# First chunk of an adaLN block: scale and shift weights in halves of 512 columns, all row tiles transposed ahead of the first query matmul, and the shift of k-tiles 0 to 3 added last, as a bias

## The chip, the cores and the metric

The kernel runs on one core of a Trainium2 chip. The metric is the device time of one execution in microseconds (us); several executions are timed, and the median is quoted. The granted clock is the TensorE clock that the chip's throttle let through, as a share of full speed; in a run at a mean of 0.998 it fell for some microseconds (3.4 in the one that was profiled). TensorE is called PE in the profile, its weight loads PEld, VectorE DVE, ScalarE ACT, GpSimd POOL, and the engine that issues the DMAs SP. SBUF is the core's working memory, PSUM the memory that TensorE writes its results to, in banks.

## The reference, cut to what matters

In an adaLN block the scale and the shift that follow a layer norm are computed from a second input, here `c`.

```python
x = A_x                                           # 2048 rows of 1024, bf16
mod = (silu(c) @ w_mod)                           # six vectors of 1024: sa, ca, ga, sb, cb, gb
h = layernorm(x) * (1 + ca) + sa                  # "scale" is 1 + ca, "shift" is sa
qkv = h @ wqkv                                    # q, k, v; linear attention follows
x = x + ga * (attention(q, k, v) @ wo)
h = layernorm(x) * (1 + cb) + sb
return x + gb * (silu(h @ w_gate) * (h @ w_up) @ w_down)
```

The opening must therefore do this before the large matmuls can run: load x and normalise it, transpose it (the contraction is over the 1024 columns), compute the scale and the shift from 2 MB of weights each, apply both, and multiply by the query weights. The first chunk is 512 rows, that is four row tiles of 128. Its 1024 columns make eight k-tiles of 128.

## The kernel before: the parts that the change and the argument touch

All DMAs of the opening are issued in order on one queue. The scale weights (`wca`) and the shift weights (`wsa`) come in pieces of 256 columns, which makes DMA rows of 512 bytes; x and the query weights have rows of 2 KB.

```python
for p in range(4):
    ca_load(p)            # 256 columns of the scale weights: 512 KB in rows of 512 B
    if p != 2:
        sa_load(p)        # 256 columns of the shift weights
    if p < 3:
        wq_load(p)        # two k-tiles of the query weights: 512 KB in rows of 2 KB
for i in range(6, 8):
    P.dma("wq%d" % i, ...)
sa_load(2)                # the shift of k-tiles 4 and 5 comes last
```

The scale and the shift are made by matmuls of one column (`mod_sc`: eight for each of the eight k-tiles, in PSUM bank 0). The opening works in halves of 256 rows: row tiles 0 and 1 are transposed, scaled and multiplied, then tiles 2 and 3.

```python
def mod_sc(w, c0, ms):
    for m in ms:
        for kt in range(NDT):
            P.pe("matmul", out=PS[:, 0, c0 + m:c0 + m + 1], lhsT=w[:, kt, m * 128:(m + 1) * 128],
                 rhs=SILUC[:, kt:kt + 1], ...)
# ...
mod_sc(WCA, 8, range(2))        # scale of k-tiles 0 and 1
warm(4, bank=3)                 # filler matmuls of 512 columns
# ...
mod_sc(WSA, 0, range(2))        # shift of k-tiles 0 and 1
warm(3, bank=3)
# ... scale and shift h of k-tiles 0 and 1 from PSUM, copy the other k-tiles unscaled to SBUF

def q_phase_chunk0(side):
    for nt in range(5):
        q_part(nt, qb[nt], (0, 1), 0, 256)      # first half of the rows
    tile_transposes(2)
    tile_transposes(3)
    for dt in range(2):
        h0_first(dt, 1, "dve")
    # ... copies; second half; then k-tiles 2 to 7, each with its own scale and shift matmuls ...
            if nt == 5:
                bias_mm()                        # shift of k-tiles 4 and 5 as a bias of q
            q_part(nt, qb[nt], (7,))
    for f in ln_ops[1]:                          # statistics of row tile 5, on VectorE
        f()
```

The last piece, the shift of k-tiles 4 and 5, is not added to h before the query matmuls. Its product with the query weights is a vector, and that is given to the activations that empty the query banks as a bias (`BIASQ`). Before the key matmuls the shift is added to h itself (`h0_shift`), and the k matmuls of chunk 0 take k-tiles 4 and 5 last.

## Time and profile before

| | before |
|---|---|
| median of the timed runs | 836.52 us (836.39 to 836.97, 3 runs) |
| span of the profiled run | 834.2 us |
| TensorE busy | 823.6 us, 99% |
| first query matmul of chunk 0 | 12.53 us |
| weights of the first key matmul of chunk 0 load at | 31.29 us |

The first fence holds lines of the page: busy time of each engine with its share of the span and its instructions, the DMA packets, and the chain that ended last by engine.

```profile
PE 823.6 (99%) x4050; PEld 380.4 (46%) x4129; DVE 304.1 (36%) x676; ACT 197.3 (24%) x339; POOL 42.9 (5%) x56
DMA packets 195085, 117.18 MB, mean 140 GB/s; under 512 B 49624, under 2 KB 178784, under 8 KB 195040
PE 97%; DVE 1%; DMA 1%; issue 1%; SPq 0%; ACT 0%; DVEq 0%
```

TensorE is nearly full, and the chain is TensorE almost everywhere. What can still be won is in the opening. The next fence is the timeline of TensorE alone in the kernel before: start in us, duration in us, engine, line, operation, tiles, shape, count, and in brackets the idle time before it with what ended it.

```profile
12.53 1.38 PE L178 MATMUL ps<-ht,wqk 128*128 128x256 bf16 x10 [0.34 <-DVE ht L178]
13.74 1.06 PE L178 MATMUL ps<-ident,xres 128*128 128x128 bf16 x16
15.09 1.04 PE L178 MATMUL ps<-ht,wqk 128*128 128x256 bf16 x6 [0.28 <-DVE ht L178]
...
24.38 0.55 PE L178 MATMUL ps<-siluc,wsa 128*128 128x1 bf16 x16
...
28.94 0.55 PE L178 MATMUL ps<-modtmp,wqk 128*128 128x1 bf16 x16
29.36 40.89 PE L178 MATMUL ps<-ht,wqk 128*128 128x512 bf16 x183
```

The 16 transposes of row tiles 2 and 3 stand between query matmuls, and TensorE then waits for their scaled copies. From 29 us on the matmuls follow each other every 0.216 to 0.220 us. The weight loads tell more than the matmuls where a wait is short, but they overstate what it costs: in a dense stretch a load stands one matmul (0.216 us) ahead of its own matmul, and a wait up to about that length costs TensorE nothing (at 29.75 us below the loads waited 0.30 us, and the matmuls still followed each other at 0.215). What is lost shows in the starts of the matmuls. This is the timeline of the weight loads before:

```profile
24.38 0.47 PEld L178 LDWEIGHTS ps<-siluc,wsa 128*128 128x128 bf16 x16 [0.53 <-DMA wsa<-in_w_mod_dram]
...
29.75 2.73 PEld L178 LDWEIGHTS ps<-ht,wqk 128*128 128x128 bf16 x14 [0.30 <-DVE biasq L178]
32.84 0.10 PEld L178 LDWEIGHTS ps<-ht,wqk 128*128 128x128 bf16 x1 [0.37 <-DVE ht L178]
33.11 0.98 PEld L178 LDWEIGHTS ps<-ht,wqk 128*128 128x128 bf16 x6 [0.17 <-DVE ht L178]
```

At 24.38 us they wait for a piece of shift weights, at 29.75 for the copy of the bias (it frees bank 0 for the eighth query group). The first eight loads from 29.75 on are that group; the ninth, at 31.29 us, is the first key matmul. At 32.84 and 33.11 us the first key group waits for the two shifted k-tiles. Its loads come every 0.216 us, so without these waits the one at 33.11 would have come at 31.29 + 7 x 0.216 = 32.80: it is 0.31 us late. The two shifts come late because they stand on VectorE behind statistics of row tile 4, which wait for ScalarE. At 46 us there is a similar wait: the first query matmuls of the second chunk need h that VectorE is scaling just then, after a DMA has transposed it.

```profile
32.12 0.22 DVE L178 SCALAR_TENSOR_TENSOR mv<-sumx,sumsq 128x1 f32<-128x1 f32 x1 [0.74 <-ACT ht L178]
...
32.45 0.61 DVE L178 TENSOR_SCALAR ht<-ht,modcol 128x512 bf16<-128x512 bf16 x2
...
44.46 2.67 DVE L178 TENSOR_SCALAR ht<-ht,modcol 128x512 bf16<-128x512 bf16 x8 [0.34 <-DMA ht<-xres]
```

```profile
47.19 1.84 PEld L178 LDWEIGHTS ps<-ht,wqk 128*128 128x128 bf16 x10 [0.23 <-DVE ht L178]
```

The last fence of before shows the traffic of the opening from 6 to 24 us: window and its length, busy time of PE, PEld, DVE, ACT and POOL with instructions, granted TensorE clock, DMA busy share, GB/s.

```profile
6.00:24.00 18.00, 17.07 (x188) 10.09 (x189) 10.28 (x44) 7.17 (x12) 2.24 (x4) 1.00 1.13 322
```

The DMA engines are busy throughout (a share above 1 means that packets overlap) and move 322 GB/s.

### The profile page before, as it was taken

Reading aid. Unit: us, or ns where it says so; the run is one execution under the profiler, and the core shown is the slowest. Engines: PE = TensorE matmul, PEld = TensorE weight load, DVE = VectorE, ACT = ScalarE, POOL = GpSimd, SP = SyncE. Lnnn points to the kernel's source line nnn. Section 1 sums busy time; section 2 is a strip of 40 time slices with the busy share of each in tenths; the row PEclk is TensorE's granted clock in tenths of the full one; section 3 lists DMA queues with packets and bytes.
Section 4 is the critical chain, followed back from the end, with each engine's and each line's share of the span. In section 5 each row is a group of like instructions: output and inputs, shape, how many; then the busy total and the mean of one; then the engine's idle time right before and its main releaser. Section 6 shows DMA issues by size and latency. Waiting matters only on the chain.

```text
span 834.2 us, 10048 instructions
## 1 busy us (share of the span) xinstructions
PE 823.6 (99%) x4050; PEld 380.4 (46%) x4129; DVE 304.1 (36%) x676; ACT 197.3 (24%) x339; POOL 42.9 (5%) x56
## 2 busy tenths in 40 slices
PE   8999999999999999999999999999999999999998
PEld 4444444454444444444444444444444444444444
DVE  6698975757974211110222212022111212111111
ACT  4568642213332111110211111011111111111011
POOL 1000000000050000030000003000000300000000
PEclk9999999999999999999999999999999999999999
DMA  9969734928197895620455571045557104553000
GB/s 278 308 151 223 213 91 146 201 101 302 26 228 227 262 281 152 169 52 19 114 152 152 151 183 45 13 114 152 152 152 193 34 13 117 154 152 95 1 26 25
DMA packets 195085, 117.18 MB, mean 140 GB/s; under 512 B 49624, under 2 KB 178784, under 8 KB 195040
## 3 DMA queue, kind: packets, MB, share of 16 engines
q1 hardware_dynamic: 195040, 116.55, 51.0%
q8 instruction: 32, 0.52, 0.3%
q14 instruction: 13, 0.11, 0.0%
HBM read 100.67 MB, written 4.33 MB: 126 GB/s over the span
## 4 chain that ended last, share of the span: by engine, by line
PE 97%; DVE 1%; DMA 1%; issue 1%; SPq 0%; ACT 0%; DVEq 0%
PE ps L178 97%; DMA wsa<-in_w_mod_dram 1%; DVE acc L178 0%; SPq L178 0%; DVE xres L178 0%; DVE mhl L178 0%; DVE ht L178 0%; ACT mw L178 0%; DVE modtmp L178 0%; DVE ve L178 0%; DVE ut L178 0%; DVE modcol L178 0%; DVE mean L178 0%; DVE msq L178 0%; DVE sumx L178 0%
## 5 line engine op out<-in xcount | busy, mean ns | idle before, releaser
L178 PE MATMUL ps<-h2t,guu 128*128 128x512 bf16 x878 | 210.1, 379 | 0.9
L178 PE MATMUL ps<-h2t,gug 128*128 128x512 bf16 x878 | 209.9, 379 | 0.9
L178 DVE TENSOR_TENSOR at<-sg,ps 128x512 bf16<-128x512 bf16 x112 | 77.0, 688 | 296.2 <-PE ps L178 285.1
L178 ACT ACTIVATE sg<-ps 128x512 bf16<-128x512 f32 x112 | 67.0, 598 | 310.2 <-PE ps L178 298.5
L178 PEld LDWEIGHTS ps<-h2t,guu 128*128 128x128 bf16 x896 | 87.7, 98 | 105.7
L178 PEld LDWEIGHTS ps<-h2t,gug 128*128 128x128 bf16 x896 | 87.5, 98 | 105.3
L178 PE MATMUL ps<-ht,wqk 128*128 128x512 bf16 (+1 forms) x510 | 112.2, 375 | 1.4 <-DVE ht L178 0.6
L178 PE MATMUL ps<-wd_a,at 128*128 128x512 bf16 (+2 forms) x519 | 112.8, 372 | 0.5
L178 PE MATMUL ps<-wd_b,at 128*128 128x512 bf16 (+2 forms) x388 | 85.4, 372 | 0.5
L178 PEld LDWEIGHTS ps<-wd_a,at 128*128 128x128 bf16 x528 | 51.1, 98 | 59.8
L178 PEld LDWEIGHTS ps<-ht,wqk 128*128 128x128 bf16 x522 | 49.8, 98 | 60.4 <-DVE ht L178 2.6
L178 DVE TENSOR_TENSOR ut<-att,gb_b 128x512 bf16<-128x512 bf16 (+1 forms) x32 | 14.0, 438 | 167.1 <-ACT att L178 167.1
L178 ACT ACTIVATE att<-ps 128x512 bf16<-128x512 f32 (+1 forms) x32 | 17.4, 591 | 182.1 <-PE ps L178 182.1
L178 PEld LDWEIGHTS ps<-wd_b,at 128*128 128x128 bf16 x396 | 38.3, 98 | 44.7
L178 PE MATMUL ps<-pk,xres 128*128 128x512 bf16 x249 | 56.2, 379 | 0.5 <-issue 0.2
L178 PE MATMUL ps<-mw,pqt 128*128 128x512 bf16 x250 | 55.8, 379 | 0.4
L178 POOL TENSOR_SCALAR h2t<-h2t,modcol 128x512 bf16<-128x512 bf16 x32 | 28.5, 909 | 393.9 <-DMA h2t<-xn 377.6
L178 ACT ACTIVATE e<-ps 128x512 bf16<-128x512 f32 x56 | 33.0, 604 | 31.4 <-PE ps L178 21.9
L178 PEld LDWEIGHTS ps<-mw,pqt 128*128 128x128 bf16 x256 | 24.9, 98 | 29.7 <-DVE xres L178 0.2
L178 PEld LDWEIGHTS ps<-pk,xres 128*128 128x128 bf16 x256 | 24.7, 98 | 29.8 <-issue 0.4
L178 ACT ACTIVATE junk<-xres 128x1024 bf16<-128x1024 bf16 x24 | 25.4, 1059 | 36.0 <-DVE xres L178 35.8
L178 POOL TENSOR_TENSOR rstd<-ve,neghalf 128x1 f32<-128x1 f32 (+2 forms) x17 | 13.7, 817 | 217.3 <-DVE ve L178 176.6
(101 smaller groups left out, 347.7 us busy)
## 6 DMA issues: line engine op xcount, KB each, us to landing
gug<-in_B_w_gate_dram SPq DMA_DIRECT2D x56, 512.0 KB, 4.0
guu<-in_B_w_up_dram SPq DMA_DIRECT2D x56, 512.0 KB, 5.3
xres<-in_A_x_dram SPq DMA_DIRECT2D x20, 256.0 KB, 6.9
rb<-recip_den SPq DMA_DIRECT2D x8, 512.0 KB, 11.4
stgx<-in_w_mod_dram SPq DMA_DIRECT2D x2, 2048.0 KB, 8.7
wd_a<-in_B_w_down_dram SPq DMA_DIRECT2D x4, 1024.0 KB, 7.5
out_dram<-xres SPq DMA_DIRECT2D x31, 128.0 KB, 1.7
xres<-in_A_x_dram SPq DMA_DIRECT2D x3, 1024.0 KB, 14.5
```

Of the source, the lines that this page charges most:

```text
L178: return getattr(e, method)(**kw)
```

## The change

The intent is to hand TensorE longer pieces of work and the DMA engines longer rows. The scale and shift weights come in halves of 512 columns (rows of 1 KB); the scale of k-tiles 0 to 3 is computed at once; all four row tiles are transposed ahead of the first query matmul; in k-tiles 0 to 3, h is first scaled only, 512 rows at a time, straight from PSUM. The shift of k-tiles 0 to 3 is loaded last and enters q as a bias, and the key matmuls of chunk 0 begin with k-tiles 4 to 7. The statistics of row tiles 4 and 5 also come earlier in the program. Cut to its core:

```diff
-        for p in range(4):
-            ca_load(p)
-            if p != 2:
-                sa_load(p)
-            if p < 3:
-                wq_load(p)
-        # ... wq 6, wq 7, sa_load(2)
+        ca_load(0)            # now 512 columns: 1 MB in rows of 1 KB
+        wq_load(0, 2)
+        ca_load(1)
+        wq_load(2, 2)
+        sa_load(1)
+        # ... wq_load(4) to wq_load(7)
+        sa_load(0)
 # (cut) bias_mm:
-                for dt in (4, 5):
+                for dt in range(4):
 # (cut) opening:
-        mod_sc(WCA, 8, range(2))
         warm(4, bank=3)
 # (cut) row tile 3: statistics wholly on VectorE instead of half on ScalarE
-        mod_sc(WSA, 0, range(2))
-        warm(3, bank=3)
+        mod_sc(WCA, 8, range(4))
+        fin_ca(0, 4)
+        tile_transposes(2, 3)
+        h0_first(0, "dve")    # 512 rows each, scale only
+        h0_first(1, "dve")
+        h0_first(2, "dve")
+        h0_first(3, "dve")
+        raw_copy(4)           # ScalarE, 1024 wide
+        raw_copy(6)
 # (cut) after the shift of k-tiles 6 and 7: act_stats(4), the statistics of row tile 4, which stood behind k-tile 7
 # (cut) k_group:
-            for i, dt in enumerate((0, 1, 2, 3, 6, 7, 4, 5) if ch == 0 else range(NDT)):
+            for i, dt in enumerate((4, 5, 6, 7, 0, 1, 2, 3) if ch == 0 else range(NDT)):
 # (cut) q_phase_chunk0, k-tile 7:
+                if nt == 0:
+                    mod_sc(WSA, 0, range(4))
+                    fin_sa(0, 4, True)
+                    for f in ln_ops[1]:
+                        f()
+                    ln1_rstd1(5)
+                if nt == 4:
+                    bias_mm()
 # (cut)
-            for dt in (4, 5):
+            for dt in range(4):
                 h0_shift(dt)
```

More of the change, by code (lines that the diff above doesn't have):

```diff
@@ L399, in ca_load, with wq_load @@
         def ca_load(p):
-            P.dma("wca%d" % p, WCA[:, :, 256 * p:256 * p + 256], wmv[:, :, D + 256 * p:D + 256 * p + 256])
-        def wq_load(p):
-            P.dma("wqp%d" % p, WQK[:, 2 * p:2 * p + 2, 0:D], wqkvv[:, 2 * p:2 * p + 2, 0:D])
+            P.dma("wca%d" % p, WCA[:, :, 512 * p:512 * p + 512], wmv[:, :, D + 512 * p:D + 512 * p + 512])
         def sa_load(p):
-            P.dma("wsa%d" % p, WSA[:, :, 256 * p:256 * p + 256], wmv[:, :, 256 * p:256 * p + 256])
-        for p in range(4):
-            ca_load(p)
-            if p != 2:
-                sa_load(p)
-            if p < 3:
-                wq_load(p)
-        for i in range(6, 8):
-            P.dma("wq%d" % i, WQK[:, i, 0:D], wqkvv[:, i, 0:D])
-        sa_load(2)
+            P.dma("wsa%d" % p, WSA[:, :, 512 * p:512 * p + 512], wmv[:, :, 512 * p:512 * p + 512])
+        def wq_load(i, n=1):
+            P.dma("wq%d" % i, WQK[:, i:i + n, 0:D], wqkvv[:, i:i + n, 0:D])
+        ca_load(0)
[3 more added lines that the diff above has]
+        sa_load(1)
+        wq_load(4)
+        wq_load(5)
+        wq_load(6)
+        wq_load(7)
+        sa_load(0)
         for j in range(2):
             P.dma("x1_%d" % j, XRES[:, 4 + j, :], xv[:, 4 + j, :])
-        for i in range(2):
+        for i in (1, 0):
             P.dma("wk0%d" % i, WQK[:, 4 * i:4 * i + 4, 1024:1536], wqkvv[:, 4 * i:4 * i + 4, 1024:1536])
@@ L508, in mod_sc, with fin_ca, fin_sa @@
                     mod_first[0] = False
-        def fin_ca(p):
-            sl, sp = slice(2 * p, 2 * p + 2), slice(8 + 2 * p, 10 + 2 * p)
-            return [
-                lambda: P.dve("tensor_copy", out=MODTMP[:, sp], in_=PS[:, 0, sp]),
-                lambda: P.dve("tensor_copy", out=MODTMP[:, sl], in_=PS[:, 0, sl]),
-                lambda: P.dve("tensor_scalar", out=MODTMP[:, sp], in0=MODTMP[:, sp], scalar1=1.0, scalar2=None,
-                              op0=ALU.add),
-                lambda: P.dve("tensor_copy", out=MODCOL[:, 1, sl], in_=MODTMP[:, sl]),
-                lambda: P.dve("tensor_copy", out=MODCOL[:, 0, sl], in_=MODTMP[:, sp]),
-            ]
-        def mv_pair(p):
-            mod_sc(WCA, 8, range(2 * p, 2 * p + 2))
-            mod_sc(WSA, 0, range(2 * p, 2 * p + 2))
-        def mod_pair(p):
-            mv_pair(p)
-            for f in fin_ca(p):
-                f()
-            for dt in range(2 * p, 2 * p + 2):
-                h0_scale(dt)
-        def h0_scale_only(dt):
-            P.dve("tensor_scalar", out=HT[:, 0, dt, :], in0=HT[:, 1, dt, :], scalar1=MODCOL[:, 0, dt:dt + 1],
-                  scalar2=None, op0=ALU.mult)
+        def fin_ca(m, n):
+            P.dve("tensor_scalar", out=MODCOL[:, 0, m:m + n], in0=PS[:, 0, 8 + m:8 + m + n], scalar1=1.0, scalar2=None,
+                  op0=ALU.add)
+        def fin_sa(m, n, cast=False):
+            if cast:
+                P.dve("tensor_copy", out=MODTMP[:, m:m + n], in_=PS[:, 0, m:m + n])
+            P.dve("tensor_copy", out=MODCOL[:, 1, m:m + n], in_=PS[:, 0, m:m + n])
         def h0_shift(dt):
@@ L541, in bias_mm, with h0_first, raw_copy @@
             for nt in range(NDT):
-                for dt in (4, 5):
+                for dt in range(4):
                     P.pe("matmul", out=PS[:, 0, 16 + nt:17 + nt], lhsT=WQK[:, dt, nt * 128:(nt + 1) * 128],
-                         rhs=MODTMP[:, dt:dt + 1], start=False, stop=(dt == 5), skip_group_check=True)
+                         rhs=MODTMP[:, dt:dt + 1], start=False, stop=(dt == 3), skip_group_check=True)
             P.dve("tensor_copy", out=BIASQ[:], in_=PS[:, 0, 16:24])
         def t_view(dt, n=1):
-            return PSB[:, 6 + dt // 4, (dt % 4) * 256:(dt % 4 + n) * 256]
-        def h0_first(dt, half, eng):
-            dst = HT[:, 0, dt, 256 * half:256 * half + 256]
+            return PSB[:, 4 + dt // 2, (dt % 2) * 512:(dt % 2 + n) * 512]
+        def h0_first(dt, eng):
             if eng == "act":
-                P.act("activation", out=dst, in_=t_view(dt), func=ACT.Identity, scale=MODCOL[:, 0, dt:dt + 1],
-                      bias=MODCOL[:, 1, dt:dt + 1])
-            else:
-                P.dve("tensor_scalar", out=dst, in0=t_view(dt), scalar1=MODCOL[:, 0, dt:dt + 1],
-                      scalar2=MODCOL[:, 1, dt:dt + 1], op0=ALU.mult, op1=ALU.add)
-        def raw_copy(dt, n, half, eng):
-            dst = HT[:, 1, dt:dt + n, 256 * half:256 * half + 256]
-            src = t_view(dt, n).rearrange("p (d q) -> p d q", q=256)
-            if eng == "act":
-                P.act("activation", out=dst, in_=src, func=ACT.Copy)
-            else:
-                P.dve("tensor_copy", out=dst, in_=src)
+                P.act("activation", out=HT[:, 0, dt, :], in_=t_view(dt), func=ACT.Copy, scale=MODCOL[:, 0, dt:dt + 1])
+            else:
+                P.dve("tensor_scalar", out=HT[:, 0, dt, :], in0=t_view(dt), scalar1=MODCOL[:, 0, dt:dt + 1],
+                      scalar2=None, op0=ALU.mult)
+        def raw_copy(dt):
+            P.act("activation", out=HT[:, 1, dt:dt + 2, :], in_=t_view(dt, 2).rearrange("p (d q) -> p d q", q=512),
+                  func=ACT.Copy)
         def h0_scale(dt):
@@ L607, in neg_rstd, with tile_transposes @@
             P.pool("tensor_tensor", out=RSTD[:, st:st + 1], in0=VE[:, st:st + 1], in1=NEGHALF[:, 0:1], op=ALU.pow)
-        def mixed_mv_ops(st):
-            return [
-                lambda: P.dve("bn_aggr", out=MV[:, st, :], in_=STATS[:, (st // 4) % 2, st % 4, 0:1, :]),
-                lambda: P.dve("scalar_tensor_tensor", out=MSQ2[:, st:st + 1], in0=MV[:, st, 0:1], scalar=MV[:, st, 0:1],
-                              in1=MV[:, st, 1:2], op0=ALU.mult, op1=ALU.add),
-                lambda: P.dve("scalar_tensor_tensor", out=MV[:, st, 0:1], in0=MV[:, st, 0:1], scalar=0.5,
-                              in1=SUMX[:, st:st + 1], op0=ALU.mult, op1=ALU.add),
-                lambda: P.dve("scalar_tensor_tensor", out=SUMSQ[:, st:st + 1], in0=MSQ2[:, st:st + 1], scalar=0.5,
-                              in1=SUMSQ[:, st:st + 1], op0=ALU.mult, op1=ALU.add),
-                lambda: P.dve("scalar_tensor_tensor", out=MV[:, st, 1:2], in0=MV[:, st, 0:1], scalar=MV[:, st, 0:1],
-                              in1=SUMSQ[:, st:st + 1], op0=ALU.mult, op1=ALU.subtract),
-            ]
         act_stats(2)
-        act_stats(3, 512)
         s0_, s1_, s3_ = ln1_stats_ops(0), ln1_stats_ops(1), ln1_stats_ops(3)
-        m2, m3 = act_mv_ops(2), mixed_mv_ops(3)
-        def tile_transposes(j):
+        m2 = act_mv_ops(2)
+        def tile_transposes(*js):
             for dt in range(NDT):
-                c = (dt % 4) * 256 + (j % 2) * 128
-                P.pe("transpose", out=PSB[:, 6 + dt // 4, c:c + 128], in_=XRES[:, j, dt * 128:(dt + 1) * 128],
-                     identity=IDENT[:])
-        fa = fin_ca(0)
+                for j in js:
+                    c = (dt % 2) * 512 + j * 128
+                    P.pe("transpose", out=PSB[:, 4 + dt // 2, c:c + 128], in_=XRES[:, j, dt * 128:(dt + 1) * 128],
+                         identity=IDENT[:])
         warm(13, bank=3)
@@ L648, in bass_adaLN_cond__linear_attn_block__swiglu_ffn__prompt_kernel @@
         tile_transposes(1)
-        warm(0, bank=3)
-        mod_sc(WCA, 8, range(2))
         warm(4, bank=3)
@@ L653, in bass_adaLN_cond__linear_attn_block__swiglu_ffn__prompt_kernel @@
         m2[0]()
-        m3[0]()
         neg_rstd(2)
-        m3[1]()
-        m3[2]()
-        fa[0]()
+        s3_[1]()
+        s3_[2]()
+        ln1_rstd1(3)
         ln1_xn(2)
-        fa[2]()
-        m3[3]()
-        fa[4]()
-        m3[4]()
-        mod_sc(WSA, 0, range(2))
-        warm(3, bank=3)
-        neg_rstd(3)
-        fa[1]()
-        raw_copy(4, 4, 0, "act")
-        fa[3]()
-        h0_first(0, 0, "dve")
-        h0_first(1, 0, "dve")
-        raw_copy(2, 2, 0, "dve")
-        ln1_xn(3)
+        ln1_xn(3)
+        mod_sc(WCA, 8, range(4))
+        fin_ca(0, 4)
+        tile_transposes(2, 3)
+        warm(0, bank=3)
+        h0_first(0, "dve")
[4 more added lines that the diff above has]
+        raw_copy(6)
+        P.act("activation", out=ACTWARM[:], in_=SILUC[:], func=ACT.Exp)
         phi_ctr = [0]
@@ L706, in phi_flush, with q_part @@
             phi_pend.clear()
-        def q_part(nt, bank, dts, c0=0, c1=512):
+        def q_part(nt, bank, dts):
             for dt in dts:
-                P.pe("matmul", out=PS[:, bank, c0:c1], lhsT=WQK[:, dt, nt * 128:(nt + 1) * 128],
-                     rhs=HT[:, 0, dt, c0:c1], start=(dt == 0 and c0 == 0), stop=(dt == 7), skip_group_check=True)
+                P.pe("matmul", out=PS[:, bank, :], lhsT=WQK[:, dt, nt * 128:(nt + 1) * 128],
+                     rhs=HT[:, 0, dt, :], start=(dt == 0), stop=(dt == 7))
         qk_ctr = [0]
@@ L769, in q_phase_chunk0 @@
         def q_phase_chunk0(side):
-            qb = [1, 2, 3, 4, 5, 6, 7]
-            for nt in range(5):
-                q_part(nt, qb[nt], (0, 1), 0, 256)
-            tile_transposes(2)
-            tile_transposes(3)
-            for dt in range(2):
-                h0_first(dt, 1, "dve")
-            raw_copy(4, 4, 1, "act")
-            raw_copy(2, 2, 1, "dve")
-            P.act("activation", out=ACTWARM[:], in_=SILUC[:], func=ACT.Exp)
-            for nt in range(5):
-                if nt == 3:
-                    mod_pair(1)
-                q_part(nt, qb[nt], (0, 1), 256, 512)
@@ L784, in q_phase_chunk0 @@
-            for nt in range(5, 7):
-                q_part(nt, qb[nt], (0, 1))
-            f2, f3 = fin_ca(2), fin_ca(3)
-            for nt in range(7):
-                if nt == 4:
-                    mod_sc(WCA, 8, range(4, 6))
-                    for i in (0, 2, 4):
-                        f2[i]()
-                    for dt in (4, 5):
-                        h0_scale_only(dt)
-                q_part(nt, qb[nt], (2, 3))
-            for nt in range(7):
-                if nt == 3:
-                    mod_sc(WCA, 8, range(6, 8))
-                    for i in (0, 2, 4):
-                        f3[i]()
-                if nt == 5:
-                    mod_sc(WSA, 0, range(6, 8))
-                    for i in (1, 3):
-                        f3[i]()
-                    for dt in (6, 7):
-                        h0_scale(dt)
-                q_part(nt, qb[nt], (4, 5))
@@ L807, in q_phase_chunk0 @@
-            for nt in range(7):
-                q_part(nt, qb[nt], (6,))
-            for nt in range(7):
-                if nt == 3:
-                    mod_sc(WSA, 0, range(4, 6))
-                    for i in (1, 3):
-                        f2[i]()
-                if nt == 5:
+            qb = [1, 2, 3, 4, 6, 5, 7]
+            for nts, dts in ((range(6), (0,)), (range(2), (1,)), ((6,), (0, 1)), (range(2, 6), (1,))):
+                for nt in nts:
+                    q_part(nt, qb[nt], dts)
@@ new lines, in q_phase_chunk0 @@
+            mod_sc(WCA, 8, range(4, 8))
+            fin_ca(4, 4)
+            for nt in range(7):
+                if nt == 6:
+                    mod_sc(WSA, 0, range(4, 6))
+                    fin_sa(4, 2)
+                    for dt in (4, 5):
+                        h0_scale(dt)
+                q_part(nt, qb[nt], (2, 3))
+            mod_sc(WSA, 0, range(6, 8))
+            fin_sa(6, 2)
+            for dt in (6, 7):
+                h0_scale(dt)
+            act_stats(4)
+            for dt in (4, 5, 6):
+                for nt in range(7):
+                    q_part(nt, qb[nt], (dt,))
@@ L815, in q_phase_chunk0 @@
+            for nt in range(7):
+                if nt == 0:
[4 more added lines that the diff above has]
+                    ln1_rstd1(5)
+                if nt == 4:
                     bias_mm()
                 q_part(nt, qb[nt], (7,))
-            for f in ln_ops[1]:
-                f()
-            ln1_rstd1(5)
-            q_phi = lambda nt: phi_evac(qb[nt] if nt < 7 else 0, PQT[:, nt, 0:512], bias=BIASQ[:, nt:nt + 1])
@@ L821, in q_phase_chunk0 @@
-            act_stats(4, mid=lambda: q_phi(0))
             for f in act_mv_ops(4):
@@ L824, in q_phase_chunk0 @@
             neg_rstd(4)
-            for i, dt in enumerate((4, 5, 0, 1, 2, 3, 6, 7)):
+            ln1_xn(5)
+            ln1_xn(4)
+            th_dma(5)
+            th_dma(4)
+            q_phi = lambda nt: phi_evac(qb[nt] if nt < 7 else 0, PQT[:, nt, 0:512], bias=BIASQ[:, nt:nt + 1])
+            for i, dt in enumerate(range(NDT)):
                 P.pe("matmul", out=PS[:, 0, :], lhsT=WQK[:, dt, 896:1024], rhs=HT[:, 0, dt, :], start=(i == 0),
                      stop=(i == 7))
-            for dt in (4, 5):
+            for dt in range(4):
                 h0_shift(dt)
             for nt in range(8):
-                if nt > 0:
-                    q_phi(nt)
+                q_phi(nt)
                 for f in side.get(nt, []):
@@ L846, in ln_x1 @@
             ln1_rstd1(4 + jj)
-        for jj in range(2):
-            add(qside, 0, lambda jj=jj: ln1_xn(4 + jj))
-            add(qside, 0, lambda jj=jj: th_dma(4 + jj))
         for f in ln_ops[2]:
```

## The prediction

> **What bounds the kernel now.** TensorE: the page's busy table gives PE 823.6 of 834.2 us (99%), the chain of waits is 97% PE. From about 29 us on, matmuls follow each other (pieces of 49 in 10.79 us, 0.220 us each), so only the first 30 us can change. A gain is how much earlier the first k matmul of chunk 0 starts; counting matmuls in the timeline puts that at about 31.6 us in before.
>
> From the first q matmul (12.53 us) to there, 19.1 us pass. 64 q matmuls are worth 64 x 0.220 = 14.1 us, 16 transposes 1.06, seven groups of 16 one-column matmuls 0.40 each = 2.8. The other 1.1 us are idle PE: for the scaled h of row tiles 2 and 3 at 14.8 us (0.28), a shift-weight DMA at 24.4 (0.53), and small ones.
>
> **What the change does.**
> - The transposes of row tiles 2 and 3 leave that interval. Tile 3's statistics go wholly to VectorE (677 ns per bn_stats of 512), its normalisation should end near 11.6 us, transposes near 12.65, first q matmul about 12.7. Saves about 1.06 + 0.3 us, less 0.15.
> - Scalings from PSUM become 512 wide: 256 wide took 406 ns, the PSUM copy of 512 415, so I estimate 0.42 to 0.50 us each, four in a row. The bank of the sixth q group is free only after the fourth: a PE gap of about 0.2 us near 14 us. The two 1024-wide ACT copies (1.01 us) just keep pace.
> - Bias over four k-tiles, not two: 16 more one-column matmuls, +0.40 us. Modulation matmuls stay 128, with 32 before the first q matmul as now.
> - DVE: four shifts instead of two (0.31 us each). k begins with k-tiles 4 to 7, so the first shifted tile is needed 0.88 us later; I expect no k wait above 0.3 us (before about 0.15).
> - DMA: bytes up to the last shift weights are unchanged (7 MB), but modulation rows go from 512 B to 1 KB. By landing times, 512 KB took about 1.72 us with 512 B rows and 1.37 with 2 KB rows. Fitted linearly per packet, 1 KB rows take 1.49 (estimate): 0.47 us saved per MB. This agrees in kind with the Trainium skill, "DMA: Bandwidth & Descriptors", section "Why small descriptors are slow (HBM only)".
>
> **Critical path after.** Estimated landings: first scale half 10.5 us, shift half for k-tiles 4 to 7 19.2 (PE wants it about 19.4), last shift half 24.9 (wanted about 25.2). Everything just fits, so PE stays nearly dense and k starts near 30.1 to 30.5 us: 1.1 to 1.5 us sooner. If 1 KB rows are no faster, these two land at 20.8 and 27.5, PE waits 2.3 us, and the kernel is slightly slower. Weighing both, I expect 1.0 us gain: **835.5 us**, range 834.6 to 837.0. Over 2% is 16.7 us, more than all the idle time of the opening. Chances: faster by over 2% 0.005, within 2% 0.99, slower 0.005.
>
> **What would show it.** Timeline: first q matmul 12.5 to 13.0 us, 16 transposes directly before; k from 30.1 to 30.5. Waits: PE on the shift weights under 0.5 us in total, on the scaled h under 0.5. DMA view: landings as above.
>
> **What would make it wrong.** Shift weights late (waits near 19 and 25 us); the PE clock falling between 10.5 and 12.7 us, when only one-column matmuls and transposes run (the Trainium skill, "TensorE: Matmul & The Clock Gate", Part 4, says transposes do not count as busy; before has filler matmuls there): q matmuls of 0.43 us would cost 1 to 2 us; VectorE late with the shifts, so the first k group waits.

## More of the kernel before

Seven query groups use banks 1 to 7. The eighth uses bank 0, so it can start only when the bias has been copied out of it.

## The result, and the profile after

The changed kernel took 835.15 us (834.89 to 835.28, 4 runs) against 836.6 us (836.39 to 836.97, 4 runs: the three of the table and one more). Ratios here are the mean time of one kernel's runs over that of the other's of the same rounds, so they are not quite the ratio of the quoted medians: 0.9982, with a 95% interval from 0.9965 to 0.9999. It is 1.45 us faster. Timed again with five runs on another occasion it took 835.2 us against 836.68 us, ratio 0.9981 (0.9968 to 0.9994).

These are the lines of the page after:

```profile
PE 821.7 (99%) x4053; PEld 379.3 (46%) x4132; DVE 301.0 (36%) x657; ACT 195.8 (24%) x335; POOL 43.2 (5%) x56
DMA packets 190940, 117.17 MB, mean 141 GB/s; under 512 B 49576, under 2 KB 174640, under 8 KB 190896
PE 96%; DMA 1%; DVE 1%; SPq 1%; issue 1%; ACT 0%; DVEq 0%
```

The packets fell by 4145; 4 MB in rows of 1 KB instead of 512 B would be 4096 fewer. The timeline of TensorE after:

```profile
11.90 1.01 PE L178 MATMUL ps<-ident,xres 128*128 128x128 bf16 x15 [0.45 <-DVE xres L178]
13.21 2.99 PE L178 MATMUL ps<-ht,wqk 128*128 128x512 bf16 x13 [0.29 <-DVE ht L178]
...
19.87 0.55 PE L178 MATMUL ps<-siluc,wsa 128*128 128x1 bf16 x16 [0.29 <-DMA wsa<-in_w_mod_dram]
...
25.75 0.94 PE L178 MATMUL ps<-siluc,wsa 128*128 128x1 bf16 x32
...
27.41 0.94 PE L178 MATMUL ps<-modtmp,wqk 128*128 128x1 bf16 x32
28.43 16.78 PE L178 MATMUL ps<-ht,wqk 128*128 128x512 bf16 x76
```

The program has 14 query matmuls in the second line and the trace 13: one record is missing. The weight loads show that the first of them began at about 12.98 us, and that nothing idles between it and 16.03 us. The weight loads after:

```profile
19.86 0.47 PEld L178 LDWEIGHTS ps<-siluc,wsa 128*128 128x128 bf16 x16 [0.78 <-DMA wsa<-in_w_mod_dram]
...
25.59 1.01 PEld L178 LDWEIGHTS ps<-siluc,wsa 128*128 128x128 bf16 x32 [0.17 <-DMA wsa<-in_w_mod_dram]
...
28.81 5.11 PEld L178 LDWEIGHTS ps<-ht,wqk 128*128 128x128 bf16 x25 [0.29 <-DVE mv L178]
```

Both halves of the shift weights are waited for, briefly. Counting eight loads of the eighth query group from 28.81 us puts the first key load at 30.37 us, 0.92 us sooner than before. The key group then runs without a break, where before its matmuls lost 0.10 us. Together that is 1.03 us, and this much is gained by 34 us. Far later stages are shifted by 1.3 us: the first matmul of the gate is at 250.6 us before and at 249.3 after, and the span falls from 834.2 to 832.9 us. The other 0.26 us are gained at 46 us. There the second chunk's weight loads came every 0.32 us before. After, the statistics of row tiles 4 and 5 are done earlier, the DMAs that transpose the second chunk are issued from 30.04 us on instead of 33.87, VectorE scales it 2.6 us sooner, and TensorE does not wait:

```profile
41.86 2.67 DVE L178 TENSOR_SCALAR ht<-ht,modcol 128x512 bf16<-128x512 bf16 x8 [0.36 <-DMA ht<-xres]
```

After 48 us the two kernels keep the same distance.

The traffic of the same window after:

```profile
6.00:24.00 18.00, 16.26 (x178) 8.98 (x180) 8.68 (x28) 5.67 (x8) 2.46 (x4) 1.00 1.08 365
```

The same DMA engines, just as full, moved 365 GB/s instead of 322. That is one of two candidate causes. The other is TensorE's own work: no transposes and no waiting for h among the query matmuls. The experiments undo each in turn. The 0.26 us at 46 us belong to neither; none of the experiments undoes them, and the traces of all twelve kernels have them (0.26 or 0.27 us).

### The profile page after: what moved, and what is told of

It reads as the page before. It is cut to its first block, busy times and chain, and to the rows that moved or that the text cites. A ratio compares the mean times of both kernels' runs of the same rounds, so it can differ in the third digit from the quotient of the medians. Undisturbed runs are those within 1.5% of the kernel's fastest.

```text
span 832.9 us, 10029 instructions
## 1 busy us (share of the span) xinstructions
PE 821.7 (99%) x4053; PEld 379.3 (46%) x4132; DVE 301.0 (36%) x657; ACT 195.8 (24%) x335; POOL 43.2 (5%) x56
## 4 chain that ended last, share of the span: by engine, by line
PE 96%; DMA 1%; DVE 1%; SPq 1%; issue 1%; ACT 0%; DVEq 0%
PE ps L178 96%; DMA wsa<-in_w_mod_dram 1%; SPq L178 1%; DVE acc L178 0%; DVE xres L178 0%; DVE mhl L178 0%; ACT mw L178 0%; DVE ve L178 0%; DVE ut L178 0%; DVE mean L178 0%; DVE msq L178 0%; DVE sumx L178 0%; DVEq L249 0%
## 5 line engine op out<-in xcount | busy, mean ns | idle before, releaser
L178 PE MATMUL ps<-ht,wqk 128*128 128x512 bf16 x499 | 110.7, 380 | 0.9 <-DVE ht L178 0.3
L178 PEld LDWEIGHTS ps<-mw,pqt 128*128 128x128 bf16 x256 | 24.9, 98 | 29.7 <-DVE xres L178 0.2
```

What stands on the lines that cost most here:

```text
L178: return getattr(e, method)(**kw)
```

## The experiments

Twelve kernels ran. The kernel before ran beside them, 836.6 to 836.7 us on each occasion. "The changed kernel" is the one above; its 835.20 us of the first group is the base for all differences, also of the kernels that ran on other occasions.

### The two causes, each undone

The first run is the changed kernel itself, with no edit.

> The changed kernel as it is, timed beside the other three on the same chip. Every theory: 1.3 to 1.5 us faster than before (about 835.15 us against 836.6), the first k matmul of chunk 0 near 30.6 us, the two waits of TensorE for shift weights together about 0.5 us.

It took 835.20 us (834.68 to 835.35, 5 runs), as expected. In this execution the matmuls of the first shift half start at 19.34 us, with no idle time of TensorE ahead of them, against 19.87 us and 0.29 us in the profile above: landings vary by some tenths of a microsecond between executions. The profiled execution is the fastest of the five, with the first key matmul at 30.22 us, against 30.58. The loads of the eighth query group waited 0.48 us here and 0.29 us there, which cost the matmuls 0.16 us and nothing.

Narrow rows, everything else as in the change:

```diff
-            P.dma("wca%d" % p, WCA[:, :, 512 * p:512 * p + 512], wmv[:, :, D + 512 * p:D + 512 * p + 512])
+            for h in (2 * p, 2 * p + 1):
+                P.dma("wca%d" % h, WCA[:, :, 256 * h:256 * h + 256], wmv[:, :, D + 256 * h:D + 256 * h + 256])
# (cut) the same for wsa
```

> The changed kernel with every half of the scale and shift weights loaded in two pieces of 256 columns (512 B rows), order of bytes unchanged. Theory (wider rows let the last shift weights land sooner, and that landing sets the start of k): the last shift piece lands near 27.5 us instead of 25.6, TensorE waits about 2 us for it, time about 837.0, that is slower than the changed kernel by 1.5 to 2.1 us and not better than before. Rival (the gain comes from TensorE's own work: no transposes between the q matmuls, no wait for the second half of h): 835.2 to 835.6, still over 1 us faster than before.

It took 837.27 us (836.62 to 838.4, 5 runs), ratio to before 1.0011 (0.9998 to 1.0025): 2.1 us slower than the changed kernel, and no better than before. One of the five runs had a granted clock of 0.998; the median of the other four is 837.13 us, 1.9 us slower. The weight loads of its timeline show where it waits:

```profile
17.47 2.27 PEld L178 LDWEIGHTS ps<-ht,wqk 128*128 128x128 bf16 x12 [0.73 <-DMA wqk<-in_A_wqkv_dram]
...
21.20 0.46 PEld L178 LDWEIGHTS ps<-siluc,wsa 128*128 128x128 bf16 x16 [0.62 <-DMA wsa<-in_w_mod_dram]
...
27.50 0.47 PEld L178 LDWEIGHTS ps<-siluc,wsa 128*128 128x128 bf16 x16 [0.62 <-DMA wsa<-in_w_mod_dram]
...
30.76 0.33 PEld L178 LDWEIGHTS ps<-ht,wqk 128*128 128x128 bf16 x3 [0.87 <-DVE mv L178]
```

The last shift piece is there at 27.50 us instead of 25.6, as the theory had it, and the traffic from 6 to 24 us is back near the old rate:

```profile
6.00:24.00 18.00, 16.39 (x178) 9.00 (x177) 8.72 (x27) 5.50 (x8) 2.46 (x4) 1.00 1.13 325
```
 
The wait at the bias copy also grew, to 0.87 us. The change without its wider rows gains nothing. By their starts the matmuls lost 0.78, 0.29, 0.26 and 0.68 us to DMAs of shift and query weights and 0.54 us at the bias copy, 2.55 us in all; in the trace after it was 0.45 us, to a DMA.

This run also doubles the number of these DMAs, from four to eight, which could be a cause of its own. The packet records of the kept traces speak for the rows. Of the packets that start from 6 to 24 us, one of 512 B took 31 ns on average (in before and in this run), one of 1 KB 50 ns (after), and one of 2 KB 90 to 95 ns. A KB thus cost a DMA engine 62 ns in packets of 512 B and 50 ns in packets of 1 KB, with the engines full in all three traces.

The old opening in halves of 256 rows, with everything else as in the change:

```diff
-            for nts, dts in ((range(6), (0,)), (range(2), (1,)), ((6,), (0, 1)), (range(2, 6), (1,))):
-                for nt in nts:
-                    q_part(nt, qb[nt], dts)
+            for nt in range(5):
+                q_part(nt, qb[nt], (0, 1), 0, 256)
+            tile_transposes(2)
+            tile_transposes(3)
+            # ... scale and copy the second half ...
+            for nt in range(5):
+                q_part(nt, qb[nt], (0, 1), 256, 512)
+            for nt in range(5, 7):
+                q_part(nt, qb[nt], (0, 1))
# (cut) scaling and copies 256 wide; statistics of row tile 3 as before
```

> The changed kernel with the old opening: row tiles 0 and 1 transposed and multiplied first, in halves of 256 rows, tiles 2 and 3 transposed between the q matmuls; loads with 1 KB rows, order and bias as in the change. Theory (landings set the start of k): first q matmul sooner, near 12.2 us, the transposes and their wait cost about 1 us in between, but that eats the waits for the shift weights; slower than the changed kernel by 0 to 0.5 us, about 835.2 to 835.7. Rival (TensorE's own work is the gain): slower than the changed kernel by 0.8 to 1.3 us, near 836.2.

It took 836.33 us, with a wide spread: 835.24, 835.5 and 836.33 us at a granted clock of 1.0, 837.04 and 837.12 us at 0.998. The profile was taken of the slowest. Its single microseconds show the cause of the 0.998 (the granted clock is the third number from the right):

```profile
13.00:14.00 1.00, 1.00 (x9) 0.81 (x9) 0.86 (x3) 0.00 (x0) 0.00 (x0) 0.77 1.10 374
14.00:15.00 1.00, 1.00 (x10) 0.87 (x9) 0.00 (x0) 0.00 (x0) 0.00 (x0) 0.50 1.06 364
15.00:16.00 1.00, 1.00 (x12) 0.96 (x9) 0.16 (x1) 0.00 (x0) 0.00 (x0) 0.50 1.08 356
16.00:17.00 1.00, 0.98 (x7) 0.48 (x5) 0.96 (x4) 0.74 (x1) 0.00 (x0) 0.53 1.09 349
```

TensorE ran at half clock: 0.46 + 1 + 1 + 0.94 = 3.4 us of it (twice what each clock misses from 1), from about 13.54 us to 16.94. The 16 transposes took 1.91 us instead of 1.06. So this run mixes two effects, and the next separates them.

Both undone, the old opening and the narrow rows (the two edits above together):

> Both undone: old opening in halves and loads in pieces of 256 columns (512 B rows), with order and bias as in the change. Theory (landings): as with the 512 B rows alone, about 837.0, since the late shift weights hide the opening entirely; difference to that kernel under 0.3 us. Rival (TensorE's own work): the opening adds its 1 us here too, so about 836.4 and near 1 us slower than with the narrow rows alone.

It took 837.43 us (836.97 to 838.36, one of five at 0.998), 0.16 us from the narrow rows alone, which is far inside the spread of either kernel. Where the weights land late, no effect of the opening is seen. It is 0.75 us slower than before (ratio 1.001, 0.9998 to 1.0023, so not clear of noise): what is left of the change, the bias over four k-tiles and the other orders, is no gain in sum.

The old opening with fillers, so that the clock holds:

```diff
+        warm(3, bank=3)
         mod_sc(WCA, 8, range(4))
+        warm(4, bank=3)
```

> The old opening in halves with 1 KB rows again, now with three filler matmuls of 512 columns ahead of the scale matmuls and four behind them, because two of five runs of the unfilled one had a granted clock of 0.998 and the profiled one fell to half clock from 13.2 to 16.9 us. Theory (landings set the start of k, the rest was the clock): granted clock 1.0 in every run, 835.2 to 835.8, at most 0.6 us slower than the changed kernel. Rival (TensorE's own work in the opening is worth about 1 us by itself): 836.0 to 836.5 even at full clock.

The granted clock was 1.0 in all five runs, and it took 835.98 us (835.78 to 836.34). That is 0.8 us slower than the changed kernel, more than the theory allowed and just below the rival's range. The unfilled kernel's three runs at full clock had a median of 835.5 us. So the new opening is worth 0.3 to 0.8 us with wide rows, and at most 0.2 us, inside the spread, with narrow ones. The table gives the four medians.

| | rows of 1 KB | rows of 512 B |
|---|---|---|
| opening with all four tiles | 835.20 | 837.27 |
| opening in halves | 835.98 (filled; 835.5 unfilled at full clock) | 837.43 |

The rows are worth 1.5 to 2.1 us, the opening 0.2 to 0.8. The 1.5 and the 0.8 compare a filled kernel with unfilled ones. Unfilled and at full clock alone, the rows are worth 1.8 to 1.9 us and the opening 0.2 to 0.3. Neither theory was right alone: landings bind where rows are narrow, and with wide rows TensorE's own work seems to show, by an amount that these runs do not fix.

### The order of the key matmuls

```diff
-            for i, dt in enumerate((4, 5, 6, 7, 0, 1, 2, 3) if ch == 0 else range(NDT)):
+            for i, dt in enumerate(range(NDT)):
```

> The changed kernel with the k matmuls of chunk 0 in the order of k-tiles 0 to 7, so that the four shifted tiles are needed first. Theory (shifting last is free only because k starts with tiles 4 to 7): the first k matmul waits for the first shift and the next ones for theirs, since VectorE makes them 0.27 to 0.31 us apart and starts them near 30.5 us; 0.5 to 0.9 us slower than the changed kernel, about 835.9. Rival (the order does not matter, the waits are hidden): 835.2, difference under 0.2 us.

It took 835.47 us (835.38 to 835.74), 0.27 us slower. The direction is as expected, the size half of it. The weight loads of the first key group wait 0.65 us and twice 0.17 us in the trace; part of that is covered by matmuls still running: by their starts the matmuls lost 0.45 us. This order is not that of the kernel before, which also took its shifted k-tiles last.

### The shift early instead of as a bias

```diff
         ca_load(0)
+        sa_load(0)
         wq_load(0, 2)
# (cut) h0_first scales and shifts; bias_mm, BIASQ and h0_shift removed
         tile_transposes(2, 3)
+        warm(2, bank=3)
+        mod_sc(WSA, 0, range(4))
+        warm(3, bank=3)
+        fin_sa(0, 4)
```

> The changed kernel without the shift as a bias: shift weights of k-tiles 0 to 3 loaded right behind their scale weights, shift added together with the scale, no bias matmuls, no shifts before k, five filler matmuls of 512 columns in the opening. Theory (the bias pays because it keeps 1 MB out of the way of the first q matmul): first q matmul near 14.8 us instead of 12.9, one wait of about 0.6 us for the second shift half near 22 us, k from about 31.4 us; 0.6 to 1.2 us slower than the changed kernel, about 836.0. Rival (the bias costs its 16 more one-column matmuls and the shifts, and buys nothing): 834.6 to 834.9.

It took 836.17 us (835.87 to 838.1; the 838.1 at a clock of 0.998), 1.0 us slower than the changed kernel. The query matmuls began at about 15 us, their weights after a wait of 0.78 us for the DMA of the query weights. The bias seems to pay by moving 1 MB of weights from ahead of the first query matmul to the end, where TensorE has other work. The run also has five more fillers, whose cost was not separated.

### No wait for shift weights

```diff
-                    mod_sc(WSA, 0, range(4, 6))
+                    mod_sc(WCA, 0, range(4, 6))
# (cut) the same for the other two; the result is wrong on purpose
```

> The changed kernel whose shift matmuls read the scale weights, long landed, so that nothing on TensorE waits for shift weights (the result is wrong on purpose; the loads stay). Theory (only landings and the bias copy keep TensorE idle by now): 0.3 to 0.7 us faster than the changed kernel, about 834.7, the granted clock 1.0. Rival (the landings no longer matter, all that is left is TensorE's work): within 0.15 us of 835.2.

It took 835.06 us (834.85 to 835.74), only 0.14 us faster. The theory's 0.3 to 0.7 us did not come. The trace shows why: two lines of VectorE and one of the weight loads.

```profile
26.76 1.29 DVE L178 BATCH_NORM_STATS2 stats<-xres 128x6 f32<-128x512 bf16 x2 [0.26 <-DMA xres<-in_A_x_dram]
...
28.40 0.16 DVE L178 COPY biasq<-ps 128x8 f32<-128x8 f32 x1
```

```profile
28.61 4.43 PEld L178 LDWEIGHTS ps<-ht,wqk 128*128 128x128 bf16 x22 [0.60 <-DVE mv L178]
```

TensorE reached the eighth query group sooner and waited 0.60 us there instead of 0.29 or 0.48; its matmuls lost 0.27 us instead of nothing or 0.16. It needs bank 0, bank 0 needs the bias copied out, and the copy stands on VectorE behind the statistics of row tile 5, which wait for that tile's DMA. The wait is put down to `mv`, the next of VectorE's instructions, but the copy is what it needs. There is a second reason: in the other trace of the changed kernel TensorE was not idle for shift weights at all, so in such an execution there was nothing to gain.

### Taking the bias copy out of the way

```diff
-                if nt == 0:
+                if nt == 2:
                     mod_sc(WSA, 0, range(4))
                     fin_sa(0, 4, True)
-                    for f in ln_ops[1]:
-                        f()
-                    ln1_rstd1(5)
+                    ln_ops[1][0]()
# (cut) the rest of the statistics after bias_mm; the four shifts before ln1_xn(5) and ln1_xn(4)
```

> The changed kernel with another order on VectorE and TensorE only: the copy of the query bias is no longer behind the statistics of row tile 5 (only their first half stays ahead of it), the four shifts come before the normalisation of tiles 4 and 5, and the last shift matmuls come after two of the seven matmuls of k-tile 7 instead of before all of them. Theory (after the change the last wait is the bias copy, which stands behind statistics that wait for row tile 5 to land): the wait of TensorE before the eighth q group falls from 0.3 to 0.5 us to under 0.1, k starts 0.3 to 0.6 us sooner, time 834.6 to 834.9. Rival (that wait is covered by something else as late): 835.1 to 835.3.

Its five runs were 834.64, 834.68, 834.89, 835.16 and 837.96 us, the last at a granted clock of 0.998. The median, 834.89 us, is 0.3 us below the changed kernel's, but the ratio to before, 0.9987 (0.9974 to 1.0), is not better than the changed kernel's 0.9981. That ratio includes the run at 0.998; the other four alone give 0.9980, still the same. The wait ahead of the eighth group is gone. A new one of 0.43 us stands before the bias matmuls, because only two query matmuls are left to cover the making of the shift vector. It cost the matmuls 0.09 us, and what was removed had cost them nothing in one trace and 0.16 us in the other, so there was little to win:

```profile
27.00 0.86 PEld L178 LDWEIGHTS ps<-modtmp,wqk 128*128 128x128 bf16 x32 [0.43 <-DVE modcol L178]
27.79 3.14 PEld L178 LDWEIGHTS ps<-ht,wqk 128*128 128x128 bf16 x16
```

The same without any wait for shift weights (wrong, edited as above):

> The reordered kernel whose shift matmuls read the scale weights (wrong result on purpose). Theory (without the bias copy in the way, the landings of the shift weights are worth what they make TensorE wait): 0.2 to 0.5 us faster than the reordered kernel, about 834.4; the earlier run without these waits gave it back at the bias copy. Rival (landings of shift weights cost nothing by now): within 0.1 us of the reordered kernel.

It took 835.02 us (834.85 to 835.81), no faster than 834.89. The rival is the better supported: no cost of the landings of the shift weights was seen. The runs of each kernel spread by 0.5 to 1 us, though, so some tenths could hide there. In the one profiled execution the scale weights landed late (the scale matmuls start at 11.08 us, 10.39 in the reordered kernel's), but the first query matmul came only 0.07 us later. In the reordered kernel's profiled execution TensorE was not idle for shift weights either.

The reordered kernel with the statistics of row tile 3 finished sooner:

```diff
         s3_[0]()
+        s3_[1]()
+        s3_[2]()
+        ln1_rstd1(3)
         ln1_xn(1)
         tile_transposes(1)
# (cut) the same three lines removed further down; ln1_xn(3) ahead of ln1_xn(2)
```

> The reordered kernel with the statistics of row tile 3 finished before tile 1 is normalised, so that the transposes of tiles 2 and 3 need not wait and the first q matmul comes sooner (near 12.4 us instead of 12.9). Theory (from there on the landings set the pace): the half microsecond comes back as longer waits for shift weights, and the time stays within 0.25 us of the reordered kernel. Rival (TensorE's own work): 0.4 to 0.6 us faster than the reordered kernel.

It took 834.99 us (834.91 to 835.78). The experiment missed its aim: the normalisation of tile 1 moved back, its transposes moved from 9.07 to 9.95 us, and the first query matmul, which comes later in TensorE's program, started at 13.20 us, not 12.4. It says nothing about the two theories.

The reordered kernel with two more fillers in the opening:

```diff
-        warm(4, bank=3)
+        warm(6, bank=3)
```

> The reordered kernel with six instead of four filler matmuls of 512 columns ahead of the scale matmuls (0.43 us more), because one of its five runs had a granted clock of 0.998 and took 837.96 us. In the trace the transposes of tiles 2 and 3 wait until 11.86 us for tile 3 anyway, 0.45 us after the first of them. Theory (the fillers fit into that wait): no cost, 834.7 to 835.1 in runs of granted clock 1.0, and no run at 0.998 of five (weak evidence: one in five was seen without them). Rival (TensorE has no slack there): 0.3 to 0.5 us slower than the reordered kernel.

It took 835.62 us (six runs: 834.7 and 834.79, and four from 835.6 to 835.74), all at a granted clock of 1.0. Four of six runs were about 0.7 us above the reordered kernel's median. Whether the fillers cost that is not shown: single runs of three kernels without them were as high at full clock (835.74, 835.81 and 835.78 us in the runs without waits for shift weights and in the one before this), and the profiled run, one of the two fast ones, does not show a cost. Why the runs fall into two groups stays open. No version was shown to beat the changed kernel.

## Why the prediction was right

The predicted time was 835.5 us with a range of 834.6 to 837.0; measured were 835.15 and later 835.20. Point by point:

- **Only the first 30 us can change: not quite.** The gain seen at 34 us is 1.03 us, that of the span 1.3. The other 0.26 us come at 46 us, where the prediction took the matmuls to be dense.
- **Wider rows: right, and the largest term.** The prediction estimated 0.47 us per MB. Undoing them cost 2.1 us; four MB at 0.47 would be 1.9, which is also what the runs at full clock alone give. The rates say the same: 325, 322 and 365 GB/s with narrow, narrow and wide rows. This was argued before the run from two durations of the trace (1.72 and 1.37 us for 512 KB) and agrees in kind with the Trainium skill, "DMA: Bandwidth & Descriptors", section "Why small descriptors are slow (HBM only)", which names a fixed cost for each packet. The mechanism inside the DMA engine is not visible in any run here.
- **Landings: near, one earlier and two later.** The scale half was expected at 10.5 us and landed at about 10.1 (issue at 3.06 plus 7.0 to landing); the two shift halves were expected at 19.2 and 24.9 us and were waited for until 19.86 and 25.59. TensorE also came later than thought, so the waits stayed short: 0.95 us in sum on the weight loads, where under 0.5 was forecast, and the matmuls had 0.29 us of idle time and were 0.45 us late by their starts; in the second trace it was 0.50 us on the loads and nothing on the matmuls.
- **First query matmul: a little late.** About 12.98 us (12.91 in the second trace) instead of 12.7; the transposes waited until 11.90 us for row tile 3.
- **Scaling from PSUM: right.** 478 ns each, predicted 420 to 500. The gap near 14 us did not come: the later start had given the four scalings time.
- **The key group: the wait right, the start a little late.** The prediction put the wait before at "about 0.15" and expected none above 0.3 after; the matmuls lost 0.10 us before and nothing after. What removed this wait was not tested alone: after, the four shifts start at 30.48 us, where the two of before started at 32.45, and the new order is needed besides, for undoing it costs 0.27 us. The first key matmul started at 31.51 us before (31.6 predicted) and at 30.58 after (30.1 to 30.5), so 0.93 us sooner, where 1.1 to 1.5 was forecast.
- **One term was missed: the second chunk.** With the 0.10 us, and with 0.26 us that the prediction had not counted, the sum is 1.29 us. That it lies in the forecast 1.1 to 1.5 us is in part luck.
- **The weighing of the two outcomes was too careful.** The prediction had 1.1 to 1.5 us if everything fits and a slight loss if 1 KB rows were no faster, and quoted 1.0. The first case came. The second is what the run with narrow rows showed: 0.6 us slower than before in the medians, though the interval of the ratio (0.9998 to 1.0025) does not exclude equality.
- **The bias: right in sign.** It costs 16 more one-column matmuls, 0.40 us, and without it the kernel is 1.0 us slower.
- **The clock: named as a danger, not met in nine timed runs of the changed kernel,** but met in six runs of its variants. Whether transposes count as busy, which the prediction worried about, no run tests: in the traced case the clock fell at 13.54 us, ahead of the transposes at 14.31.

What the prediction did not see is the chain behind the landings: statistics of row tile 5, bias copy, eighth query group. It is one reason why removing the last waits for shift weights gained only 0.14 us. It cannot be the only one, for with the chain out of the way their removal gained nothing either.

## What to carry to other kernels

In an opening that loads as fast as the DMA engines allow, look at the bytes that must land before each step, and at the row length of each piece; a wider piece can be worth more than all the reordering on the compute engines, even if it brings some data later than it was needed before. A vector that enters linearly can be taken out of the operand and added at the end as a bias, which makes its weights the last to load. When a wait is removed and the time stays, look for the engine on whose program the next step stands behind unrelated work, and check that the removed wait had delayed the busy engine at all: a weight load that waits is not yet a matmul that comes late.

## What the Trainium skill lacked or had wrong

- "DMA: Bandwidth & Descriptors", in the table at its top, gives 512 B and more as the smallest transfer for line rate. Here plain DMAs from HBM to SBUF were not at the rate they can reach with 512-byte rows: with a full queue, a mix of 512-byte and 2 KB rows moved 322 and 325 GB/s, and the same bytes with 1 KB rows in place of 512-byte ones 365 GB/s. The packets show it one by one: a KB took 62 ns in packets of 512 B and 50 ns in packets of 1 KB. The page has no rate of a full queue for rows of these sizes on this chip.
- "TensorE: Matmul & The Clock Gate", Part 1, warns of idle gaps above about 3.4 us, and in a second passage of short but frequent idling between groups of matmuls, for which it gives no size. In the opening in halves the clock fell to half for 3.4 us, the length of the page's window (3413 ns), although no idle gap of TensorE from 8.9 us on was above 0.80 us. In the 3.4 us ahead of the fall at 13.54 us stood the end of the fillers (to 10.38 us), 32 one-column matmuls between gaps of 0.65 and 0.80 us, and query matmuls from 12.78 us on. The page gives no measure of how much work in a window is enough. Seven fillers of 512 columns around the scale matmuls kept five of five runs at a granted clock of 1.0, against three of five without them. Runs at 0.998 were 1.0 to 3.2 us above the median of the same kernel's others.
